# Eight chunks of the feed-forward block in pairs: wider up matmuls, and a Strassen down product with its outputs turned by VectorE

## The chip, the cores and the metric

The kernel runs on one core of one Trainium2 chip. The time is the device time of one execution in microseconds (us). A core has TensorE (PE, matrix products; its loads of stationary data are listed as PEld), VectorE (DVE), ScalarE (ACT), GpSimd (POOL) and SyncE (SP), which here issues every DMA transfer. Each engine works through its own list of instructions in the order of the program; between engines they wait for one another through semaphores. PSUM is the memory that TensorE writes to; the kernel uses it as four pairs of banks, each tile a pair [128, 2, 512].

## What is computed

The reference is a recurrent attention block followed by a feed-forward block, all in float32:

```python
# r, k, v, w, a, b: (B, H, S, D) = (4, 8, 768, 40)
for t in range(S):
    y[:, :, t] = r_t @ state                       # per batch and head, state is 40 x 40
    Sa = state @ a_t
    state = state * w_t - outer(Sa, b_t) + outer(v_t, k_t)
x = y.transpose(0, 2, 1, 3).reshape(3072, 320)     # tokens x (heads * D)
h = x @ w_in                                       # w_in: 320 x 2048
g = h / (1 + exp(-1.702 * h))
out = g @ w_out                                    # w_out: 2048 x 320
```

The two products of the last block are called up (x @ w_in) and down (g @ w_out).

## The kernel before

The sequence is cut into 12 chunks of 64 time steps. A chunk with one half of the batch (two of the four batch rows) is a unit, so there are 24 units. For a unit, `decay`, `prep`, `inverse` and `solve` turn the recurrence over 64 steps into small matmuls. The slowest part is `inverse`: five levels, each a group of matmuls into `ps_level` (L752), a copy of the result to W by ACT or DVE (L763), a subtraction to E by DVE (L765), a 32x32 block transpose to ES by DVE (L714), and a spread of ES into EX (L719 and L721, on ACT, DVE or POOL), from which the next level's matmuls read. The state goes from chunk to chunk.

When both units of a chunk are done, its outputs go through a DRAM tile and come back as xT (320 features on partitions, 256 tokens in the free direction). Then `mlp` (L987) does the chunk's feed-forward part. *Up*: w_in is stationary, the 256 tokens move; a result tile holds two blocks of 128 hidden features, and one ACT instruction (L1000) applies the gelu to all of it and writes g. *Down*: 64 tokens of g are stationary, 320 columns of w_out move, accumulated over 16 blocks of 128 hidden features; the two banks hold the partial sums of the two partition halves, and ACT or DVE copies the first to ob (L1024), DVE adds the second (L1026), and SP sends 64 rows of 1280 bytes per transfer (L1023). Every matmul uses one 64x64 quadrant of TensorE, and `QUARTERS` lists the four quadrants, so that four matmuls form a group. `mm` (L303) issues every matmul, `transfer` (L333) every DMA; so all matmuls have the line L303 and all transfers L333 in the profile.

Nothing is scheduled by the framework. `Plan.add` records tasks with the engines that may take them and their estimated cost in ns, their reads, writes and buffers. A planner that is not part of the file has put them into one order, which stands in the source as the text `ORDER`: each word is a task's number, its engine (p, a, d, g, s) and its PSUM pair. `Plan.listed` (L89) checks that order against the dependencies and issues the tasks in it. The order within each engine, and the engine of each task, are therefore fixed in the text. Feed-forward matmuls stand between the matmuls of the recurrence.

Buffers that matter here: `g` has 4 slots (one chunk: 4 pieces q), `xT` 3, `ob` 1; `extra` is the place through which the raw weights come in at the start, and is free afterwards.

## Time and profile before

| | |
|---|---|
| runs of the kernel before (three) | 680.79, 684.27, 687.98 us; median 684.27 |
| the profiled execution: span, first to last instruction | 680.9 us |
| instructions in the profile | 42,186 |
| DMA | 69.73 MB in 35,312 packets, mean 102 GB/s |
| mean granted TensorE clock over the span | 0.987 |

The profile is of one execution, whose time is its span; outside of it the page shows nothing. The median of the runs is 3.4 us above that span. "Busy" is the time in which an engine had at least one instruction under way; matmuls are pipelined, so that a busy PE is not necessarily a full one. The chain of waits starts at the last instruction and goes back step by step to whatever released it. A group of instructions is given with its line, engine, operation, output and inputs, shape and count, then its busy time in us, the mean ns of one, and the idle time before it with what ended most of that. Each float32 matmul of the program leaves two records, so PE's x19488 are 9,744 matmuls.

### The profile page before, as it was taken

To read this page: it belongs to the slowest core of one execution; us is meant where nothing else is said; L and a number is where in the kernel's file an instruction comes from. 1 tells how busy PE (TensorE), PEld (TensorE's weight loads), DVE (VectorE), ACT (ScalarE), POOL (GpSimd) and SP (SyncE) were. 2 spreads that over 40 slices of the span, in tenths; PEclk is the share of its full clock that TensorE was granted. 3 is DMA by queue.
4 is the path that set the end of the run, shared out by engine and by line. 5 is a ranking of instruction groups with operands and counts; after the bars stand their busy time and mean duration, and the time that the engine had idled before them with its cause. 6 is when DMAs were issued, how large, how long until landed. Compare 5 with 4: busy or idle time off the path is not lost.

```text
span 680.9 us, 42186 instructions
## 1 busy us (share of the span) xinstructions
PE 651.5 (96%) x19488; PEld 561.8 (83%) x19488; DVE 452.8 (66%) x912; ACT 328.9 (48%) x682; POOL 175.4 (26%) x204
## 2 busy tenths in 40 slices
PE   5677999999999999999999999999999999999997
PEld 4666998787999788888888898798888799898785
DVE  5686789767867758858776687768666766675001
ACT  3665845644554754574445455455354354262110
POOL 5442345224123223223213221222412320300000
PEclk9977999999999999999999999999999999999999
DMA  7875563415314414432404513513412411200100
GB/s 218 275 245 148 180 203 110 142 42 152 110 36 130 129 33 120 125 115 71 126 13 126 150 38 108 153 35 106 145 33 70 121 53 42 73 13 23 51 12 20
DMA packets 35312, 69.73 MB, mean 102 GB/s; under 512 B 5440, under 2 KB 14656, under 8 KB 35136
## 3 DMA queue, kind: packets, MB, share of 16 engines
q1 hardware_dynamic: 35136, 67.03, 32.7%
q8 instruction: 153, 2.51, 1.5%
q14 instruction: 23, 0.19, 0.1%
HBM read 59.15 MB, written 7.86 MB: 98 GB/s over the span
## 4 chain that ended last, share of the span: by engine, by line
PE 90%; DMA 5%; DVE 2%; ACT 1%; issue 1%; SPq 1%; ACTq 0%; DVEq 0%
PE ps_up L303 30%; PE ps_down L303 30%; PE ps_level L303 8%; PE ps_y L303 5%; PE ps_B L303 4%; PE ps_X L303 3%; PE ps_N L303 2%; PE ps_rz L303 1%; PE ps_RV L303 1%; PE ps_A L303 1%; DMA w_sb<-in_w_in 1%; PE ps_zT L303 1%; PE ps_cum L303 1%; DMA rv<-in_rv 1%; DMA b<-in_b 1%
## 5 line engine op out<-in xcount | busy, mean ns | idle before, releaser
L303 PE MATMUL ps_up<-xT_all,w_sb 64*64 64x256 f32 x3840 | 249.4, 377 | 0.2 <-PE ps_rz L303 0.2
L303 PE MATMUL ps_down<-w_sb,g 64*64 64x320 f32 x3072 | 239.7, 430 | 0.2 <-ACT zr L881 0.2
L303 PEld LDWEIGHTS ps_up<-xT_all,w_sb 64*64 64x64 f32 x3840 | 168.3, 133 | 15.7 <-PE ps_rz L303 0.3
L303 PEld LDWEIGHTS ps_down<-w_sb,g 64*64 64x64 f32 x3072 | 135.5, 133 | 36.7 <-ACT zr L881 0.4
L1000 ACT ACTIVATE g<-ps_up 128x1024 f32<-128x1024 f32 x48 | 49.2, 1024 | 46.1 <-PE ps_up L303 45.6
L721 POOL TENSOR_TENSOR EX<-ES,quads 128x512 f32<-128x512 f32 x30 | 39.7, 1325 | 118.2 <-DVE ES L714 78.4
L763 ACT COPY W<-ps_level 128x512 f32<-128x512 f32 x56 | 32.7, 585 | 66.8 <-PE ps_level L303 65.2
L303 PEld LDWEIGHTS ps_level<-W,EX 64*64 64x64 f32 x2560 | 57.7, 134 | 6.2 <-DVE T L842 0.2
L765 DVE TENSOR_TENSOR E<-two,ps_level 128x256 f32<-128x256 f32 x80 | 33.1, 415 | 34.4 <-ACT W L763 29.7
L303 PE MATMUL ps_level<-W,EX 64*64 64x64 f32 (+1 forms) x2560 | 54.6, 217 | 0.0
L719 ACT ACTIVATE EX<-ES,quads 128x256 f32<-128x256 f32 x82 | 37.2, 501 | 31.7 <-DVE ES L714 31.3
L303 PEld LDWEIGHTS ps_level<-PT,EX 64*64 64x64 f32 x1280 | 32.0, 144 | 12.0 <-DVE EX L735 3.5
L631 POOL TENSOR_TENSOR ak<-ak,FT 128x512 f32<-128x512 f32 x17 | 22.1, 1299 | 76.7 <-DMA ak<-in_ak 49.8
L303 PE MATMUL ps_level<-PT,EX 64*64 64x64 f32 (+2 forms) x1280 | 34.0, 240 | 7.4 <-DVE EX L735 5.0
L714 DVE STREAM_TRANSPOSE ES<-E 128x256 f32<-128x256 f32 x80 | 35.3, 443 | 4.4
L303 PE MATMUL ps_y<-M,bh 64*64 64x104 f32 (+1 forms) x768 | 35.9, 252 | 1.1 <-issue 0.8
L303 PE MATMUL ps_y<-RV,kh 64*64 64x104 f32 (+1 forms) x768 | 36.2, 253 | 0.7 <-DVE M L919 0.5
L903 ACT COPY B<-ps_B 128x416 f32<-128x416 f32 (+1 forms) x35 | 17.2, 492 | 33.4 <-PE ps_B L303 33.2
L303 PEld LDWEIGHTS ps_y<-RV,kh 64*64 64x64 f32 x768 | 29.2, 137 | 3.2 <-DVE M L919 1.3
L919 DVE TENSOR_TENSOR M<-ps_X,later 128x832 f32<-128x832 f32 (+1 forms) x24 | 23.9, 994 | 11.3 <-PE ps_X L303 10.5
L303 PEld LDWEIGHTS ps_y<-M,bh 64*64 64x64 f32 x768 | 27.8, 137 | 1.8 <-issue 1.2
L303 PE MATMUL ps_B<-RV,A 64*64 64x104 f32 (+1 forms) x768 | 28.5, 250 | 0.4 <-issue 0.3
(133 smaller groups left out, 1085.3 us busy)
## 6 DMA issues: line engine op xcount, KB each, us to landing
ak<-in_ak SPq DMA_DIRECT2D x48, 160.0 KB
rv<-in_rv SPq DMA_DIRECT2D x48, 160.0 KB
time<-in_time SPq DMA_DIRECT2D x24, 320.0 KB
xT_all<-x_dram SPq DMA_DIRECT2D x48, 160.0 KB
wc<-in_wc SPq DMA_DIRECT2D x20, 264.0 KB
logw<-in_w SPq DMA_DIRECT2D x24, 160.0 KB
RV<-in_v SPq DMA_DIRECT2D x24, 160.0 KB
b<-in_b SPq DMA_DIRECT2D x48, 80.0 KB
```

Source lines behind the costliest of these rows:

```text
L303: nc.tensor.matmul(o, lhsT, rhs, start=start, stop=True, skip_group_check=True)
L631: plan.add(R, {"DVE": 690.0, "POOL": 1270.0, "sbuf": True}, lambda t: of(t.engine).tensor_mul(ahT(), ahT(), FT_of(i)), reads=T("ak", "FT") ...
L714: plan.add(rank, dve(256), lambda t: nc.vector.transpose(ES(n), source(t)), writes=[key("ES", n, 6)], **reads)
L719: nc.scalar.activation(dst[:, :, h], ES(n), ACT.Copy, scale=quads[:, h, :1])
L721: of(t.engine).tensor_mul(dst, ES(n).unsqueeze(2).to_broadcast([128, 8, 2, 32]), quads.unsqueeze(1).to_broadcast([128, 8, 2, 32]))
L763: plan.add(rank, any2(512), lambda t: copy(t.engine)(tiles_of(W(n + 1)), blocks(psum(t, ""), 64)), writes=[key("W", n + 1, 5)], pair=pair)
L765: plan.add(rank, dve(256), lambda t: nc.vector.tensor_sub(tiles_of(E(n + 1)), every(two32, [128, 2, 4, 32]), blocks(psum(t, ""), 64)[:, :, ...
L903: plan.add(R, any2(4 * wide), lambda t: copy(t.engine)(dst(), some(psum(t, "")[:, :, :208])), writes=[("Bv", i)] if x and c > 0 else T("B" ...
L919: plan.add(R + 1, dve(8 * wide), lambda t: nc.vector.tensor_tensor(M_of(i)[:, :, :wide].rearrange("p (j b) n -> p b j n", b=2), some(psum( ...
L1000: plan.add(-45, {"ACT": 1030.0, "table": "gelu"}, lambda t: nc.scalar.activation(g_of(c * NQ + q).rearrange("p m r n -> p r m n"), psum(t, ...
```

## The change

Chunks 3 to 10 are taken in pairs (3, 4), (5, 6), (7, 8) and (9, 10); chunks 0, 1, 2 and 11 are done singly as before.

- *Up* (`rise`): in a pair the two chunks' 512 tokens move past the same stationary block of w_in, in one matmul of 512 columns; a result tile holds one block of 128 features for two chunks, and the number of gelu instructions is the same.
- *Down* (`fast_down`): w_out is stationary and the tokens move, so that the result comes out with output columns on partitions. The 256 first output columns (two blocks of 128), the 1,024 + 1,024 hidden features and the two chunks' 256 + 256 tokens form 2x2 blocks, and the product of these is done in Strassen's scheme in Winograd's form: seven products of blocks (P1 to P7) in place of eight. It needs four sums of blocks of w_out, made once (`w_sums`, in `extra`), and four sums of blocks of g for every pair (T1 to T4, in place in g, four pieces each). Partial sums that are wanted on the way (e1, e3, U2, U3, W) are taken out of PSUM while the next product goes on accumulating in the same place. The last 64 output columns (`outer`, P0) are an ordinary product for both chunks.
- The five result tiles [128, 256] of a pair are combined (`combine`), turned by DVE in 32x32 blocks into places of g that are no longer needed, and sent with eight transfers each, every one with 32 partitions of 4 pieces of 32 numbers (128 bytes).
- g becomes one tile with 8 slots, ob has 2 slots, Y is new; `loose` lets a task of the pair of banks wait for its first matmul only, with its other dependencies given by name; the scratch for dynamic DMA is made smaller.
- `ORDER` is a new text for all tasks. In it some of the recurrence's tasks stand on another engine than before.

The diff, without ORDER and cut to its core:

```diff
+    GROUPS = [(0,), (1,), (2,), (3, 4), (5, 6), (7, 8), (9, 10), (11,)]
...
-                     A=1, B=1, RV=2, E0=2, W0=2, P21=2, PT=2, W=2, E=2, ES=2, EX=2, T=2, Tc=1, QT=1, zraw=2, zT=1, M=2, x=1, xT=3, g=4, ob=1), 4)
+                     A=1, B=1, RV=2, E0=2, W0=2, P21=2, PT=2, W=2, E=2, ES=2, EX=2, T=2, Tc=1, QT=1, zraw=2, zT=1, M=2, x=1, xT=3, g=8, Y=1, ob=2), 4)
...
+    w_sums = extra[:, :4 * NF * 64].rearrange("p (k q f n) -> p k q f n", k=4, q=NQ, f=2)
+    Y_more = extra[:, 4 * NF * 64:4 * NF * 64 + 4 * 256].rearrange("p (k n) -> p k n", k=4)
+    w_part = lambda m, n: w_out_sb.rearrange("p (q m f n) -> p q m f n", q=NQ, m=2, f=2)[:, :, m, :, 128 * n:128 * n + 128]
...
     def weights():
         for n in range(len(raws)):
             weight(n, RANKS[n], w_in[n] if n < NQ else w_out[n - NQ])
+
+        every = [("weight", n) for n in range(len(raws)) if n >= NQ or raws[n] in "ab"]
+        for k, (fn, one, two) in enumerate((("add", w_part(0, 1), w_part(1, 1)), ("subtract", w_sums[:, 0], w_part(0, 0)),
+                                            ("subtract", w_part(0, 0), w_part(0, 1)), ("subtract", w_part(1, 0), w_sums[:, 1]))):
+            plan.add(50, {"DVE": 1240.0, "POOL": 2500.0, "sbuf": True}, lambda t, k=k, fn=fn, one=one, two=two: of(t.engine).tensor_tensor(
+                out=w_sums[:, k], in0=one, in1=two, op=getattr(ALU, fn)),
+                     reads=every + ([("wsums", k - 1)] if k == 1 else [("wsums", 1)] if k == 3 else []), writes=[("wsums", k)])
...
-    g_of = lambda n: buf("g", n, [128, 2, 2, 256])
+    g_all = single("g_all", [128, plan.slots["g"], 2, 2, 256])
+    g_turn = {c: c for one in GROUPS for c in one}
+    for one in GROUPS:
+        if len(one) == 2 and (one[0] % 3 < one[1] % 3) != (one[0] % 2 == 0):
+            g_turn[one[0]], g_turn[one[1]] = one[1], one[0]
+    turn_of = {c: n for n, one in enumerate(GROUPS) for c in one}
+    g_no = lambda c, q: g_turn[c] * NQ + q
+    g_of = lambda n: g_all[:, n % plan.slots["g"]]
...
+    def rise(group):
+        c, both = group[0], len(group) == 2
+        R = 10000 + 100 * c
+        xs = [("xs", (n, p)) for n in group for p in BITS]
+        x_at = sorted(n % 3 for n in group)
+        x_of = lambda k: xT_all[:, x_at[0]:x_at[-1] + 1:max(1, x_at[-1] - x_at[0])].rearrange("p s (q k n) -> p s q k n", q=2, n=128)[:, :, :, k]
+        spots = lambda q: sorted(g_no(n, q) % plan.slots["g"] for n in group)
+        g_to = lambda q: g_all[:, spots(q)[0]:spots(q)[-1] + 1:max(1, spots(q)[-1] - spots(q)[0])]
+
+        def up(q, m, k):
+            at, pair = (0, ("up", (c, q, m))) if both else (m * 256, ("up", (c, q, 0)))
+
+            def go(t):
+                ph, x = psum(t, "ps_up"), x_of(k)
+                for r, h in QUARTERS:
+                    mm(ph[HALF[h], r, at:at + 256 * len(group)].rearrange("p (s q n) -> p s q n", q=2, n=128),
+                       w_in_sb[HALF[r], 2 * q + m, k, h * 64:(h + 1) * 64], x[HALF[r]], at == 0 and k == 0)
+            plan.add(R + q, pe((1, 256 * len(group))), go, reads=xs + [("weight", q)],
+                     uses=[("xT", n) for n in group], room=[("g", g_no(n, q)) for n in group], pair=pair, most=1)
+
+        def gelu(q, m):
+            def go(t):
...
+                if both:
+                    nc.scalar.activation(g_to(q)[:, :, m].rearrange("p s r n -> p r s n"), ps.rearrange("p r (s n) -> p r s n", s=2), ACT.Gelu_apprx_sigmoid)
+                else:
+                    nc.scalar.activation(g_to(q)[:, 0].rearrange("p m r n -> p r m n"), ps.rearrange("p r (m n) -> p r m n", m=2), ACT.Gelu_apprx_sigmoid)
+            plan.add(-45, {"ACT": 1030.0, "table": "gelu"}, go, writes=[("g", g_no(n, q)) for n in group],
+                     pair=("up", (c, q, m)))
...
+        for q in range(NQ):
+            for m in BITS:
+                for k in range(NK):
+                    up(q, m, k)
+                if both:
+                    gelu(q, m)
+            if not both:
+                gelu(q, 0)
...
-        def up(q, m, k):
-            def go(t):
-                ph, x = psum(t, "ps_up"), xT_of(c)[:, :, k]
-                for r, h in QUARTERS:
-                    mm(ph[HALF[h], r, m * 256:(m + 1) * 256], w_in_sb[HALF[r], 2 * q + m, k, h * 64:(h + 1) * 64], x[HALF[r]],
-                       m == 0 and k == 0)
-            plan.add(R + q, pe((1, 256)), go, reads=[("xs", (c, p)) for p in BITS] + [("weight", q)],
-                     uses=[("xT", c)], room=[("g", c * NQ + q)], pair=("up", c * NQ + q), most=1)
-
-        def gelu(q):
-            plan.add(-45, {"ACT": 1030.0, "table": "gelu"}, lambda t: nc.scalar.activation(
-                g_of(c * NQ + q).rearrange("p m r n -> p r m n"), psum(t, "").rearrange("p r (m n) -> p r m n", m=2),
-                ACT.Gelu_apprx_sigmoid), writes=[("g", c * NQ + q)], pair=("up", c * NQ + q))
-
...
-        for q in range(NQ):
-            for m in BITS:
-                for k in range(NK):
-                    up(q, m, k)
-            gelu(q)
...
+    def fast_down(c, serial):
+        R = 10000 + 100 * c
+        no = lambda q: (g_no(c, q), g_no(c + 1, q))
+        block = lambda k, n: lambda q: g_of(no(q)[n])[:, k]
+        B11, B12, B21, B22 = block(0, 0), block(0, 1), block(1, 0), block(1, 1)
+        raw = lambda m, n: lambda q: w_part(m, n)[:, q]
+        made = lambda k: lambda q: w_sums[:, k, q]
...
+        Y = lambda k: ob_of(2 * turn_of[c] + k)[:, :256] if k < 2 else buf("Y", serial, [128, 256]) if k == 2 else Y_more[:, k - 3]
+        outs = [("Y", serial), *(("ob", 2 * turn_of[c] + p) for p in BITS)]
...
+        def add(q, key, dst, one, two, reads):
+            plan.add(-46, {"DVE": 697.0, "POOL": 1290.0, "sbuf": True}, lambda t: of(t.engine).tensor_sub(dst(q), one(q), two(q)),
+                     reads=[*of_g(q), *((x, (c, q)) for x in reads)], writes=[(key, (c, q))])
+
+        def times(rank, name, at, left, right, reads, q):
+            def go(t):
+                ps = psum(t, "ps_down")
+                for f in BITS:
+                    for r, h in QUARTERS:
+                        mm(ps[HALF[h], r, 256 * at[1]:256 * at[1] + 256], left(q)[HALF[r], f, h * 64:(h + 1) * 64], right(q)[HALF[r], f],
+                           name == "P1" and q == 0 and f == 0)
+            plan.add(R + rank + 0.1 * q, pe((2, 256)), go, reads=[*of_g(q), *((x, (c, q) if x[0] == "T" else c) for x in reads), *(ready if q == 0 else [])],
+                     writes=[(name, (c, q)), (name, c)], pair=(at[0], c), loose=True, most=1)
+
+        def outer(q, m):
+            def go(t):
...
+                        n = 4 * q + 2 * m + f
+                        mm(ps[HALF[h], r, 256:512], w_out_sb[HALF[r], n * DM + 256:(n + 1) * DM], g_of(no(q)[h])[HALF[r], m, f],
+                           q == 0 and m == 0 and f == 0)
+            plan.add(R + 8 + 0.1 * q, pe((2, 256)), go, reads=[*of_g(q), *(ready if q == 0 else [])], writes=[("P0", (c, q)), ("P0", c)],
+                     pair=("dz", c), loose=True, most=1)
...
+        def evacuate(name, at, k, last, onto=None):
+            ps = lambda t, r: psum(t, "")[:, r, 256 * at[1]:256 * at[1] + 256]
+            if onto is None:
+                plan.add(-45, any2(256), lambda t: copy(t.engine)(Y(k), ps(t, 0)), reads=[(last, c), *ready], room=outs,
+                         writes=[(f"{name}0", c)], pair=(at[0], c), loose=True)
+            else:
+                plan.add(-45, dve(256), lambda t: nc.vector.tensor_add(Y(k), ps(t, 0), Y(k)), reads=[(last, c), (onto, c)],
+                         writes=[(f"{name}0", c)], pair=(at[0], c), loose=True)
+            plan.add(-45, dve(256), lambda t: nc.vector.tensor_add(Y(k), ps(t, 1), Y(k)), reads=[(f"{name}0", c)],
+                     writes=[(name, c)], pair=(at[0], c), loose=True)
+
+        def combine(name, k, fn, one, two, reads):
+            plan.add(-45, {"DVE": 436.0, "POOL": 750.0, "sbuf": True}, lambda t: of(t.engine).tensor_tensor(out=Y(k), in0=Y(one), in1=Y(two), op=fn),
+                     reads=[(x, c) for x in reads], writes=[(name, c)])
+
+        s1, s2, s3, s4 = ("dx", 0), ("dx", 1), ("dz", 0), ("dz", 1)
+        each = range(NQ)
+        for q in each:
+            for m in BITS:
+                outer(q, m)
+            times(10, "P1", s1, raw(0, 0), B11, [], q)
+        for q in each:
+            times(9, "P3", s3, made(3), B22, [], q)
+            times(11, "P2", s2, raw(1, 0), B21, [], q)
+        evacuate("M3", s4, 4, "P0")
+        evacuate("e3", s3, 5, "P3")
+        evacuate("e1", s1, 0, "P1")
+        for q in each:
+            add(q, "T1", B12, B12, B11, ["P0"])
+            times(12, "P5", s3, made(0), B12, ["T1", "e3"], q)
+            add(q, "T2", B22, B22, B12, ["T1", "P3"])
+            times(13, "P6", s1, made(1), B22, ["T2", "e1"], q)
+        evacuate("C11", s2, 0, "P2", "e1")
+        evacuate("U2", s1, 1, "P6")
+        for q in each:
+            add(q, "T3", B11, B22, B11, ["T2", "P1"])
+            times(14, "P7", s1, made(2), B11, ["T3", "U2"], q)
+        evacuate("W", s3, 6, "P5")
+        evacuate("U3", s1, 2, "P7")
+        for q in each:
+            add(q, "T4", B21, B21, B22, ["T2", "P2"])
+            times(15, "P4", s1, raw(1, 1), B21, ["T4", "U3"], q)
+        combine("C12", 1, ALU.add, 1, 6, ["U2", "W"])
+        combine("D", 2, ALU.subtract, 2, 5, ["U3", "e3"])
+        combine("C22", 2, ALU.add, 2, 6, ["D", "W"])
+        evacuate("C21", s1, 3, "P4")
+        ty = lambda k: (B22(3) if k == 4 else B12(3 - k // 2))[:, k % 2]
+        places = [("C11", 0, 0, 0), ("C12", 1, 0, 1), ("C22", 2, 1, 1), ("C21", 3, 1, 0), ("M3", 4, 2, None)]
+        for n, (name, k, block_of, chunk) in enumerate(places):
+            plan.add(-45, dve(256), lambda t, k=k: nc.vector.transpose(ty(k), Y(k)), reads=[(name, c), ("P5", c), ("P6", c), *((x, (c, q)) for x in ("T2", "T3", "T4") for q in each)],
...
+            def store(t, k=k, block_of=block_of, chunk=chunk):
+                for a in range(4):
+                    at_c, col = (c + chunk, 128 * block_of + 32 * a) if chunk is not None else (c + a // 2, 256 + 32 * (a % 2))
+                    for h in BITS:
+                        at_s = at_c * C + 32 * h
+                        to = out.rearrange("(g s) d -> s g d", g=4)[at_s:at_s + 32, :, col:col + 32]
+                        transfer(t, to, ty(k)[32 * a:32 * a + 32].rearrange("p (g h i) -> p g h i", g=4, i=32)[:, :, h])
+            plan.add(-100, {"SP": 2800.0}, store, reads=[("t" + name, c)], uses=[*of_g(2), *of_g(3)], size=128 * 256 * 4)
...
-            mlp(i // 2)
+            for group in GROUPS:
+                if group[-1] == i // 2:
+                    rise(group)
+                    if len(group) == 2:
+                        fast_down(group[0], [one for one in GROUPS if len(one) == 2].index(group))
+                    else:
+                        mlp(group[0])
...
-    nc = bacc.Bacc("TRN2", target_bir_lowering=False, num_devices=1)
+    nc = bacc.Bacc("TRN2", target_bir_lowering=False, num_devices=1, dynamic_dma_scratch_size=1024)
```

291 lines of the change are left out of this document (147 added, 144 removed).

## The prediction

> **What bounds the kernel now.** I read the profile page first: who is busy, and who ends last.
>
> ```profile
> PE 651.5 (96%) x19488; PEld 561.8 (83%) x19488; DVE 452.8 (66%) x912; ACT 328.9 (48%) x682; POOL 175.4 (26%) x204
> ...
> PE 90%; DMA 5%; DVE 2%; ACT 1%; issue 1%; SPq 1%; ACTq 0%; DVEq 0%
> PE ps_up L303 30%; PE ps_down L303 30%; PE ps_level L303 8%; PE ps_y L303 5%; PE ps_B L303 4%; PE ps_X L303 3%; PE ps_N L303 2%; PE ps_rz L303 1%; PE ps_RV L303 1%; PE ps_A L303 1%; DMA w_sb<-in_w_in 1%; PE ps_zT L303 1%; PE ps_cum L303 1%; DMA rv<-in_rv 1%; DMA b<-in_b 1%
> ```
>
> TensorE carries 90% of the chain that ended last, and the two products that the change rewrites carry 30% each. A busy PE need not be a full one, so I went on to the chain in order of time, and to the engines in equal stretches.
>
> ```profile
> 657.75 4.32 PE ps_up L303 x80
> 662.07 14.02 PE ps_down L303 x208
> ```
>
> ```profile
> 0.00:100.00 100.00, 76.89 (x2488) 71.02 (x2492) 72.10 (x116) 58.12 (x139) 42.17 (x64) 0.91 0.69 213
> ...
> 200.00:300.00 100.00, 100.00 (x3091) 85.83 (x3087) 73.57 (x147) 56.70 (x121) 28.76 (x28) 1.00 0.34 101
> 300.00:400.00 100.00, 100.00 (x3052) 84.31 (x3047) 70.79 (x149) 51.18 (x93) 24.41 (x28) 1.00 0.33 98
> 400.00:500.00 100.00, 100.00 (x3100) 86.84 (x3096) 71.53 (x151) 47.94 (x103) 25.14 (x27) 1.00 0.34 102
> ```
>
> The chain gives undisturbed prices. Each matmul in the program is two records, and four of them (one per 64x64 quadrant) run side by side: one group is eight records. So an up group of 256 columns takes 4.32/10 = 0.432 us and a down group of 320 takes 14.02/26 = 0.539 us. The slope is 0.107/64 = 1.67 ns per column and the fixed part 4 ns: nothing is to be had from fewer, longer matmuls, only from fewer columns. The stretches (columns: length, PE, PEld, DVE, ACT, POOL, granted clock, DMA share, GB/s) show PE full from 100 us on at clock 1.00. Summing the starts of successive groups against these prices, PE lost some 36 us before 75 us, while the first transfers land, and only 7 us in all the rest. DVE, the next engine, stands at 71 to 74%. So the kernel is bound by matmul columns from 75 to 676 us, and what is taken from PE there shows at once, as long as DVE keeps up.
>
> **The change on PE.** Per pair of chunks, before: 2 chunks x 2 halves x 16 groups of 320 columns = 64 x 0.539 = 34.5 us of down. After: seven products of 8 groups and the 64 outer columns as 16 groups, 72 groups of 256 = 72 x 0.432 = 31.1 us. That is 3.4 us saved, 13.6 us for four pairs. Up: 80 groups of 256 become 40 of 512; at 4 + 512 x 1.67 = 0.860 us each they save 4 ns per merged group, 160 groups: 0.6 us. The other matmuls are the same in number and shape. Both orders begin alike (PE's first 120 rows, DVE's first 114, SP's first 60), so the 36 us of the start stay, and both end with a single chunk's down and the same last store. **PE: minus 14.2 us**, if it stays fed.
>
> **The change on DVE.** The rows to price it with:
>
> ```profile
> L721 DVE TENSOR_TENSOR EX<-ES,quads 128x512 f32<-128x512 f32 x29 | 20.1, 695 | 0.9
> ...
> L965 DVE TENSOR_TENSOR x<-zr,FT 128x128 f32<-128x128 f32 x56 | 20.1, 418 | 0.2
> ...
> L636 DVE TENSOR_TENSOR ak<-ak,GT 128x512 f32<-128x512 f32 x12 | 11.0, 920 | 2.6 <-DMA ak<-in_ak 2.5
> ```
>
> ```profile
> L714 DVE STREAM_TRANSPOSE ES<-E 128x256 f32<-128x256 f32 x80 | 35.3, 443 | 4.4
> L765 DVE TENSOR_TENSOR E<-two,ps_level 128x256 f32<-128x256 f32 x80 | 33.1, 415 | 34.4 <-ACT W L763 29.7 <-PE ps_level L303 3.8
> ```
>
> New on DVE, by the changed order: 57 of the 64 subtractions T1 to T4 (128x512, as EX: 0.695) 39.6 us; 36 additions out of PSUM and 3 copies (128x256, as E: 0.415) 16.2; 20 transposes (0.443) 8.9; 5 combinations (as E) 2.1; four sums of weights (128x1024, twice EX) 5.6. Gone: 16 additions and 8 copies of ob (0.483 and 0.490), 11.6. Together +61 us. The new order also moves old work from POOL and ACT to DVE: EX spreads 29 to 65 (+25.0), x 56 to 92 (+15.0), ak products 19 to 31 (+11.0), T spreads 6 to 11 (+3.7), the rest about -20 (40 small copies of Tc at 0.214 and 7 of W at 0.682 go to ACT, among others). Together +35. DVE goes **from 453 to some 549 us**, and POOL's instructions from 204 to 147.
>
> Where it lies decides. The chunks' pairs stand between PE's work marks 50 and 525 us (marks count matmul time alone; 525 is the last matmul of the recurrence, which stood at 571 before, so it is also packed closer). In this stretch I priced every instruction by its row's median, in the order in which the program lists them over all engines. That order can be trusted for this: in the trace of before, DVE's instructions start within about a microsecond of the place it gives them. Between the marks PE has 475 us of work and DVE 456 us, 96%. In before it was 521 and 383, 73%. Cut into 25 us of PE work, DVE has more than PE in seven pieces of nineteen (27.8, 25.3, 27.4, 26.8, 25.4, 27.0, 27.7), in sum 12 us more; in before no piece exceeds 21.3. Each such piece is a wait of PE, because the recurrence (matmul, copy, transpose, spread, next matmul) runs through DVE and PE's queue is in order: behind a level's matmul that waits for its EX stand the up and down groups that would have filled the gap. Pieces of 50 us, as if engines could run far ahead, leave 3 us; pieces of 10 us 18, of 5 us 30 (before: 0, 1, 3). **I take +12**, since before's DVE never ran more than about a microsecond ahead, but waits of a few hundred ns did vanish. Bounds 3 and 30.
>
> **The stores.** A pair's outputs now leave as 40 transfers of 32x4x32 in place of 8 of 64x320, all on SP's queue.
>
> ```profile
> L333 SPq DMA_DIRECT2D out<-ob x48: 467/564/1412, 118.7 to 677.7; - x48
> ```
>
> At 0.564 us each (minimum, median, maximum in the row) a burst holds SP for 22.6 us. Queued behind it: after the first pair the loads of rv, ak and b, with 10 to 33 us of PE work until their first use; after the second pair logw and wc of a later unit, with 10 us, so they come some 4 us late to ACT's logarithm, and the gelus behind that on ACT come late with it; after the last pair, the turned outputs lie in buffers of g that the last chunk's gelus want back 22 to 25 us of PE work after the first store, just about when the last has landed. A new shape may be issued faster (loads of 40 rows: 0.29) or slower; from 0.6 us on each further 0.1 us costs the end 4 us. **I take +2**, bounds 0 and 10. Each transfer is made of 128-byte pieces, 20,480 in all; the mean piece of before costs an engine 101 ns (32.7% of 16 x 680.9 us over 35,136 pieces), which would be 32 us of each engine per pair, no more than its idle share (DMA 0.34) in the 100 us that a pair lasts. A page speaks against these stores: the Trainium skill, "DMA: Bandwidth & Descriptors", Specifications, asks for 512 bytes or more per piece for line rate, and says that smaller ones are read, modified and written. No run here shows it yet; by the rows above it would be rival C. Where the sum takes the page at its word, +2 becomes +10.
>
> **Sum.** 680.9 - 14.2 + 12 + 2 = 680.7 us for the profiled span. The runs of before lie at 680.79, 684.27 and 687.98, so the span of the profile is at their lower end, 3.4 us (0.5%) under the median; against the median the sum gives **684 us, no change**. About 1% (6.8 us) is what a measurement of this kernel tells from no change.
>
> **Rivals.**
> A, *DVE's backlog spreads out*: neighbouring pieces with room absorb it, as the 50 us pieces allow (3 us), and SP is fast enough. For it: PE lost only 7 us in 600 so far, and DVE's total still fits. Against it: before had a quarter of DVE free, here 4%. 684 - 14.2 + 3 = **673 us**.
> B, *DVE becomes the bound of the middle*: at 96% asked for, it cannot lose time to its own waits on PE and ACT. It decides from the point where DVE's busy share of the stretch falls under 456/489 = 93%: from there the waits exceed the 14.2 us gained. No stretch of the trace has DVE above 79% (39.6 of the 50 us from 100 to 150). With the 5 us pieces: 684 - 14.2 + 30 = **700 us**.
> C, *the stores*: their small pieces or their issue delay loads and the last chunk's gelus, 684 - 14.2 + 12 + 10 = **692 us**.
> That PE's saving itself fails would need groups of 512 or of the turned products to cost more than linear; the counts are fixed by the program and both forms are plain moving columns, so I give it no chance of its own.
>
> **How the numbers follow.** Forecast 0.44 (677.5 to 691), A 0.28, B 0.21, C 0.07. Faster by over 1% is A, 0.28; within it 0.44; slower B and C, 0.28. The range must reach into A and B until a tenth is out on each side: 670 to 699.
>
> **What the next profile would show.** ps_down groups at 0.432 us and fewer of them, ps_up at 0.860, and PE's sum 14 us smaller: the first step. DVE near 549 us, over 90% busy in stretches between 100 and 560 us, with PE idle there put down to DVE (EX, ES, T, the additions of L1118): the second; PE full throughout would make A right. SP's row for out<-g_all at about 0.56 us, and a last gelu that waits for out<-g_all or not: the third. The forecast is wrong if DVE's busy time is well off 549, if PE loses under 5 or over 20 us in the middle, or if the new start differs from the old.

## The result and the profile after

The changed kernel takes 730.2 us (median of four runs, 726.45 to 731.61) where the kernel before takes 683.97 on the same chip: 1.065 times as long, 95% interval 1.059 to 1.071. The forecast was 684 with a range from 670 to 699. In what follows, "over before" is (ratio - 1) x 684 us; the change stands at **+44.5 us** (40 to 49) on that scale.

The page of the changed kernel: busy time of each engine, and the chain that ended last by engine and by line.

```profile
PE 662.3 (91%) x18464; PEld 495.3 (68%) x18464; DVE 518.7 (71%) x1044; ACT 330.6 (45%) x719; POOL 121.9 (17%) x147
...
PE 73%; DVE 9%; ACT 5%; DMA 4%; issue 4%; SPq 4%; POOL 0%; ACTq 0%; DVEq 0%
PE ps_down L300 24%; PE ps_up L300 23%; PE ps_level L300 7%; PE ps_y L300 4%; PE ps_B L300 4%; SPq L330 4%; PE ps_X L300 2%; PE ps_N L300 2%; DMA b<-in_b 1%; PE ps_rz L300 1%; DVE g_all L1086 1%; PE ps_RV L300 1%; ACT W L771 1%; PE ps_A L300 1%; DVE ES L722 1%
```

TensorE's part of the chain fell from 90% to 73%. The rest is now spread over VectorE (9%), ScalarE, transfers and SP's queue (4%, 1% before). The prices of TensorE's groups are as forecast; the chain's end shows them undisturbed (start, length, what):

```profile
688.33 2.16 PE ps_up L300 x40
690.49 0.86 PE ps_down L300 x16
691.35 2.16 PE ps_up L300 x40
```

Five groups of 256 columns in 2.16 us are 0.432 each, two of a turned product in 0.86 are 0.43, and six groups of 512 columns in a row from 645.7 us on took 5.15 us, 0.858 each. So TensorE got its 14 us less of work, and lost far more. The two kernels between 100 and 600 us, before first (columns: length, PE, PEld, DVE, ACT, POOL, granted clock, DMA share, GB/s):

```profile
100.00:600.00 500.00, 498.51 (x15310) 426.95 (x15306) 358.40 (x740) 252.29 (x514) 131.96 (x139) 1.00 0.31 93
```

```profile
100.00:600.00 500.00, 462.04 (x13564) 350.22 (x13559) 397.66 (x822) 243.52 (x529) 75.63 (x77) 0.99 0.33 90
```

PE stands still for 38 of the 500 us, although VectorE is at 80% only, and no 50 us of the trace has it above 88%. Busy time still flatters PE. With the prices of its groups, each stretch can be split into up and down products, recurrence products, and time lost (us, to about 2 us):

| stretch | before: up and down, recurrence, lost | changed |
|---|---|---|
| 75 to 150 | 49.6, 22.4, 3.1 | 40.1, 25.7, 9.3 |
| 150 to 250 | 64.0, 33.9, 2.1 | 53.6, 35.3, 11.0 |
| 250 to 350 | 64.8, 34.4, 0.8 | 56.9, 36.0, 7.0 |
| 350 to 450 | 66.0, 33.5, 0.5 | 55.0, 28.7, 16.3 |
| 450 to 550 | 64.6, 33.3, 2.2 | 53.6, 28.9, 17.4 |
| behind the recurrence's last matmul | 47.5 | 78.5 |
| in all | 413.6, 214.5 | 399.3, 214.5 |

Two things stand in it. First, the losses of 350 to 550 us are large, and much of them sits in two places. TensorE's longest waits between 75 us and the end (engine, line, waited for; us in all, times, longest):

```profile
PE ps_N L300 <- DVE ak L639: 6.8, 1, 6.8
PE ps_B L300 <- ACT zr L889: 6.1, 1, 6.1
```

The first one in stretches of 5 us, with the columns as above:

```profile
390.00:395.00 5.00, 4.46 (x80) 1.87 (x80) 2.06 (x7) 2.74 (x7) 0.00 (x0) 1.00 0.22 31
395.00:400.00 5.00, 0.13 (x4) 0.00 (x0) 0.00 (x0) 0.00 (x0) 0.00 (x0) 0.91 0.45 138
400.00:405.00 5.00, 3.08 (x57) 2.19 (x61) 2.97 (x7) 0.37 (x1) 0.00 (x0) 0.50 0.07 19
405.00:410.00 5.00, 5.00 (x152) 4.00 (x148) 2.97 (x7) 3.04 (x10) 1.29 (x1) 0.91 0.08 20
```

All engines are empty from 395 to 400 us. SP had been sending a pair's outputs from 371.5 to 395.2 us, 40 transfers in a row; only then did it issue the load of ak, which landed at 400.4, and the recurrence went on. When PE came back, its granted clock was 0.50. The second stop, at 505 us, is the same with wc. Secondly, the losses begin at 75 us, where no pair's output exists yet: there each stretch has some 10 us less of up and down products in it, and 31 us of them (78.5 - 47.5) are found behind the recurrence's last matmul. (The expectation of e10 below goes by 36.6 and 77.5 us, which leaves out the first block of each.) In the kernel before, the recurrence's last matmul starts at 628.4 us, and from 628.64 up and down products run without a stop to 676.09 us; the chain of before begins that stretch with these:

```profile
628.64 10.78 PE ps_down L303 x160
639.42 4.32 PE ps_up L303 x80
643.73 2.15 PE ps_down L303 x32
```

### The profile page after: what moved, and what is told of

It is laid out like the page before. It is cut to its first block, busy times and chain, and to the rows that moved or that the text cites. A ratio compares the mean times of both kernels' runs of the same rounds, so it can differ in the third digit from the quotient of the medians.

```text
span 729.3 us, 40391 instructions
## 1 busy us (share of the span) xinstructions
PE 662.3 (91%) x18464; PEld 495.3 (68%) x18464; DVE 518.7 (71%) x1044; ACT 330.6 (45%) x719; POOL 121.9 (17%) x147
## 4 chain that ended last, share of the span: by engine, by line
PE 73%; DVE 9%; ACT 5%; DMA 4%; issue 4%; SPq 4%; POOL 0%; ACTq 0%; DVEq 0%
PE ps_down L300 24%; PE ps_up L300 23%; PE ps_level L300 7%; PE ps_y L300 4%; PE ps_B L300 4%; SPq L330 4%; PE ps_X L300 2%; PE ps_N L300 2%; DMA b<-in_b 1%; PE ps_rz L300 1%; DVE g_all L1086 1%; PE ps_RV L300 1%; ACT W L771 1%; PE ps_A L300 1%; DVE ES L722 1%
## 5 line engine op out<-in xcount | busy, mean ns | idle before, releaser
L300 PE MATMUL ps_up<-xT_all,w_sb 64*64 64x256 f32 (+1 forms) x2560 | 247.6, 488 | 3.7 <-issue 3.5
L300 PEld LDWEIGHTS ps_up<-xT_all,w_sb 64*64 64x64 f32 x2560 | 104.4, 134 | 48.2 <-issue 35.0
L300 PE MATMUL ps_down<-w_sb,g_all 64*64 64x320 f32 x1024 | 81.3, 431 | 0.9 <-issue 0.6
L300 PE MATMUL ps_down<-g_all,w_sb 64*64 64x256 f32 x1280 | 80.4, 377 | 0.9 <-issue 0.7
L300 PE MATMUL ps_down<-g_all,extra 64*64 64x256 f32 x1024 | 64.3, 378 | 4.9 <-DVE extra L1118 2.7
L771 ACT COPY W<-ps_level 128x512 f32<-128x512 f32 x63 | 36.6, 585 | 61.0 <-PE ps_level L300 57.3
L300 PEld LDWEIGHTS ps_down<-g_all,w_sb 64*64 64x64 f32 x1280 | 49.3, 133 | 16.1 <-issue 3.1
L300 PEld LDWEIGHTS ps_down<-w_sb,g_all 64*64 64x64 f32 x1024 | 45.4, 133 | 15.8 <-issue 1.8
L1026 ACT ACTIVATE g_all<-ps_up 128x1024 f32<-128x1024 f32 x32 | 32.7, 1024 | 49.1 <-PE ps_up L300 42.2
L1086 DVE TENSOR_TENSOR g_all<-g_all 128x512 f32<-128x512 f32 x57 | 40.8, 740 | 18.6 <-PE ps_down L300 18.3
L300 PEld LDWEIGHTS ps_down<-g_all,extra 64*64 64x64 f32 x1024 | 40.0, 133 | 18.3 <-DVE extra L1118 3.2
L729 DVE TENSOR_TENSOR EX<-ES,quads 128x512 f32<-128x512 f32 x65 | 47.6, 732 | 1.6
L300 PE MATMUL ps_y<-RV,kh 64*64 64x104 f32 (+1 forms) x768 | 36.6, 255 | 2.1 <-issue 1.6
```

The costliest lines, as they stand in the source:

```text
L300: nc.tensor.matmul(o, lhsT, rhs, start=start, stop=True, skip_group_check=True)
L729: of(t.engine).tensor_mul(dst, ES(n).unsqueeze(2).to_broadcast([128, 8, 2, 32]), quads.unsqueeze(1).to_broadcast([128, 8, 2, 32]))
L771: plan.add(rank, any2(512), lambda t: copy(t.engine)(tiles_of(W(n + 1)), blocks(psum(t, ""), 64)), writes=[key("W", n + 1, 5)], pair=pair)
L1026: nc.scalar.activation(g_to(q)[:, :, m].rearrange("p s r n -> p r s n"), ps.rearrange("p r (s n) -> p r s n", s=2), ACT.Gelu_apprx_sigmoid)
L1086: plan.add(-46, {"DVE": 697.0, "POOL": 1290.0, "sbuf": True}, lambda t: of(t.engine).tensor_sub(dst(q), one(q), two(q)), reads=[*of_g(q), ...
```

## The experiments

The theories, as they stood ahead of the first four: *stores* (SP's bursts make the two stops), *vector* (VectorE's longer queue makes the many small ones), *grain* (the 512-column groups hold others up), *order* (TensorE's order leaves the recurrence no time, whatever VectorE does).

### One transfer for each turned tile; subtractions made small; both; up in two halves

```diff
# e1
-                for a in range(4): ...  for h in BITS: transfer(t, to, ty(k)[32 * a:32 * a + 32]...[:, :, h])
+                transfer(t, out[n * S + c * C:n * S + c * C + 128, :256], ty(k))     # fifth tile: [128, 4, 64]
# e2
-  of(t.engine).tensor_sub(dst(q), one(q), two(q))
+  of(t.engine).tensor_sub(dst(q)[:, :, :4], one(q)[:, :, :4], two(q)[:, :, :4])
# e3: both
# e4, in the pairs
-  mm(ph[HALF[h], r, at:at + 256 * len(group)]..., x[HALF[r]], ...)
+  for s in range(len(group)): mm(ph[HALF[h], r, at + 256 * s:at + 256 * s + 256]..., x[HALF[r], s], ...)
```

Expected of e1:

> Edit: each turned tile of a pair goes out in one transfer of 128 pieces of 1 KB (the fifth: of 256 bytes), 5 transfers a pair in place of 40, to places of the output that are not the right ones; all arithmetic stays. Store theory: SP's bursts of 23.7 us (40 transfers of 0.43 us and the gaps between them, in the changed kernel's trace) cause the two long stops of TensorE at 394 and 504 us, 6.8 and 6.3 us of waiting, each followed by some 5 us at a granted clock of 0.50, so 9.5 + 8.4 us, and part of what follows at 524 us (3 us) and 355 us (3 us): 730 falls to 706 to 714 and both stops go. Vector theory: the stores are a symptom, the time stays within 3 us of 727.

Expected of e2:

> Edit: the 64 subtractions of Strassen's scheme on GELU's outputs (T1 to T4) are made on 8 of their 512 columns; the work left out is the rest of these subtractions. Everything keeps its place. Vector theory: VectorE's queue is the cause of the 45 us of small stops of TensorE between 100 and 700 us; 57 subtractions of 0.74 us there become some 0.07 us, 38 us less on VectorE, which takes its sum back to 480 from 519 us: 730 falls to 700 to 712. Store theory: no more than 5 us of it, since SP's bursts keep their place. Order theory (TensorE's order as written leaves the recurrence no time, whatever VectorE does): within 5 us of 730.

Expected of e3:

> Both edits together: one transfer for each turned tile, and the subtractions on 8 of 512 columns (the rest of them left out). If stores and VectorE are the two causes, the sum of both gains: 680 to 692. If either one alone is the cause, this equals the better of the two runs within 4 us. Order theory: stays above 700.

Expected of e4:

> Edit: in the pairs the up product goes out as two matrix products of 256 columns in place of one of 512, with the same weights loaded for each; same tasks in the same places. Grain theory (long products hold up what stands behind them, or the 512-column form itself waits): some 10 us or more are won back. Vector and store theories: the price alone, 4 pairs x 64 groups x (0.864 - 0.860 us), under 2 us either way, and TensorE's loads grow by 1280 of 0.134 us, which lie beside its products.

| | us | ratio, 95% interval | over before |
|---|---|---|---|
| changed kernel | 730.2 | 1.065 (1.059 to 1.071) | +44.5 |
| e1, one transfer a tile | 703.4 | 1.029 (1.023 to 1.036) | +20.0 |
| e2, small subtractions | 716.9 | 1.051 (1.045 to 1.056) | +34.5 |
| e3, both | 698.0 | 1.022 (1.017 to 1.028) | +15.0 |
| e4, up in halves | 733.5 | 1.074 (1.069 to 1.080) | +50.8 |

In e1 both long stops are gone; VectorE does the same work as before the edit (page, and TensorE's longest wait after 75 us):

```profile
PE 657.0 (93%) x18464; PEld 488.5 (69%) x18464; DVE 518.2 (73%) x1044; ACT 330.7 (47%) x719; POOL 121.9 (17%) x147
```

```profile
PE ps_down L300 <- DVE extra L1118: 2.7, 1, 2.7
```

So the way in which the outputs were stored costs 24.5 us (about 6 either way, from the two intervals). The gain is a little larger than the store theory's 706 to 714. The subtractions are worth 10 us by themselves, but 5 on top of e1 (the intervals of e1 and e3 overlap): 31 us of VectorE's time (518 to 487) for 5 us, far from what the vector theory asked. None of the three expectations of e2 holds: 716.9 lies between the 712 of the vector theory and the 725 that the two others allow. Grain falls: halving the groups brings nothing back (a pair has 40 of them, not the 64 of the expectation). And e3's 698.0 meets none of its three expectations, if narrowly: it is not the 680 to 692 us of two causes that make up the whole, it is 5 and not 4 us from e1, and it is not above 700. 15 us over before (11 to 19) stay, where 14 less than before were due. 29 us had no owner yet, and e3's table looked like that of the changed kernel up to 250 us (6.6 and 10.2 us lost, with 42.2 and 52.6 us of up and down products).

### The recurrence nearly alone

A new theory, *pace*: the recurrence is a chain of steps through TensorE, ScalarE and VectorE, and needs nearly all the time that it has. Up and down products between its steps are then almost free, and those behind its end cost their full length.

```diff
# e5, kernel before; e6 likewise, with times() at q == 0, f == 0 and outer() at q == m == f == 0
-  for r, h in QUARTERS:                                  # up
+  for r, h in QUARTERS if k == 0 else []:
-  for f in (2 * m, 2 * m + 1):                           # down
+  for f in (2 * m, 2 * m + 1)[:m == 0]:
```

Expected of e5:

> Edit on the kernel before: the up product takes the first of its five parts of the input features alone, the down product the first of 16 blocks of the hidden features; four fifths of the up products and fifteen sixteenths of the down products are left out, about 359 of the 414 us that up and down hold on TensorE at full rate. All else, GELU, copies and stores too, stays, and so does the order. What is left is the recurrence at its own pace. Pace theory (the recurrence's chain of VectorE, ScalarE and TensorE steps needs nearly the time that it has, so taking products from between its steps brings little): its last product, at 628 us in the kernel before, comes at 540 us or later, and the run takes 560 us or more. Filling theory (TensorE's work sets the time and the chain has ample slack): the run falls to the sum of VectorE's work and the start, 480 us or less.

Expected of e6:

> The same on the changed kernel: one fifth of the up products, one eighth of the down products of the pairs (one sixteenth of the turned one) and one sixteenth of the others are made, the rest is left out; all work of VectorE, ScalarE and the stores stays. Pace theory: the last recurrence product, at 644 us in the changed kernel, comes at 570 us or later and the run takes over 590 us, that is 20 us or more longer than the kernel before under the same cut, by the load of VectorE (519 for 453 us) and the bursts of stores. If VectorE and the stores cost the recurrence nothing by themselves, both cut kernels end within 10 us of each other.

Measured: 599.5 us (0.882, 0.875 to 0.888) for the kernel before and 669.3 us (0.984, 0.975 to 0.994) for the changed one. 359 of TensorE's us were taken from the kernel before, and 80 came back. The last recurrence matmul moved from 628 to 573 us, and from 644 to 623 in the changed kernel. VectorE, with nothing to hold it up but the chain itself (e5, then e6):

```profile
100.00:200.00 100.00, 68.21 (x2210) 55.30 (x2207) 82.09 (x168) 58.34 (x121) 33.48 (x35) 0.81 0.39 114
200.00:300.00 100.00, 72.17 (x2406) 60.10 (x2402) 77.33 (x161) 58.25 (x121) 29.99 (x28) 0.81 0.34 104
```

```profile
100.00:200.00 100.00, 72.24 (x2232) 60.58 (x2232) 84.52 (x167) 54.78 (x124) 23.64 (x23) 0.69 0.40 116
200.00:300.00 100.00, 70.69 (x2237) 56.80 (x2227) 79.50 (x169) 52.82 (x117) 14.55 (x15) 0.78 0.30 94
```

It gets to 77 to 85% in these stretches. That is not a limit of VectorE: in e3 it was busy for 45.85 of the 50 us from 100 to 150. One reservation: the granted clock fell to 0.81 and 0.69 to 0.78 here, so the recurrence's own matmuls ran slower than in the full kernels, and 573 us is more than the chain needs at full clock. The two later edits at the kernel before do not have this fault (clock 0.99 and 1.00).

```diff
# e11: e6 with the edits of e1 and e2
```

Expected:

> The changed kernel with its up and down products cut as in the earlier cut run (669 us), and in addition one transfer for each turned tile and the subtractions on 8 of 512 columns; the rest of these is left out. The kernel before under the same cut takes 599 us. If stores and subtractions are what made the recurrence of the changed kernel slower, 605 to 625. If it is rather the wait of a pair's products for both chunks and the work behind the last step (48 us behind it here, 26 in the kernel before), 640 or more.

Two executions, 620.1 and 629.7 us, and no interval: the first lies in the range of the store and subtraction theory, the second between the two. By the first, the stores and the subtractions are 49 of the 70 us between the two cut kernels, by the second 40; 21 to 30 us are left. Behind the last recurrence matmul e11 has 28 us in the profile of its longer execution (600 to 628), e5 26 (573 to 599); so nearly all of what is left is time that the recurrence itself takes longer in the new order, with few products in it and at a lower clock (0.78 for 0.82). What in the new order does that was not tried.

### Steps back on their old engines; stores on GpSimd

```diff
# e7, on e3: 258 words of ORDER, for example
-  ... 503d ... 567d ...
+  ... 503a ... 567g ...
# e8, on the changed kernel: 20 words of ORDER from s to g, and
-  transfer(t, to, ty(k)[32 * a:32 * a + 32]...)
+  nc.gpsimd.dma_start(to, ty(k)[32 * a:32 * a + 32]...)
```

Expected of e7:

> Edit on the kernel with one transfer a tile and the subtractions on 8 of 512 columns (the rest of them left out; 698.0 us): in addition the 258 small steps of the recurrence that the new order gives to another engine than the old one go back to the old one, at the same places of the order (56 from VectorE to GpSimd, 76 from VectorE to ScalarE, the others from ScalarE or GpSimd). Moved-work theory: VectorE loses some 35 us, and of the 29 us that still part 698 from 684 - 14 = 669 some 10 to 20 come back: 678 to 688. Pace theory (less of the up and down products stands between the recurrence's steps, since a pair waits for both its chunks): within 6 us of 698, either way, since the steps of the chain are as long as before or longer on GpSimd (1.33 for 0.73 us).

Expected of e8:

> Edit on the changed kernel: the 40 transfers of a pair's outputs are issued by GpSimd (17% busy) in place of SP; same transfers, same places of the order. If it is SP's time that the transfers cost (and not their 128-byte pieces), the two long stops go and 730 falls to 702 to 712, as with one transfer a tile (703.4). If it is the small pieces at the DMA engines or in memory, it stays above 722. Rival: issuing costs GpSimd so much that the recurrence's steps on it (122 us) come late: above 730.

e7 takes 724.7 us (1.065, 1.059 to 1.071), 29 us more than e3: neither theory's figure. Its last recurrence matmul comes at 637 us instead of 611. But the edit took little off VectorE, 480 us for 487 in e3 where 35 us less had been expected: 132 steps left it and 108 others came to it, and what stayed got slower (the 40 scans 908 ns for 684, b 825 for 707) with GpSimd busy for 185 us in place of 114. So the run does not decide whether the load on VectorE was the harm. It shows that, at the places of the new order, the new engines are better by 29 us than the old ones. The steps that moved to GpSimd take longer there (EX 1.31 us for 0.72), and VectorE's share of the chain that ended last went from 12% to 22%, GpSimd's from 0% to 2%; which of the 258 steps did it was not tried.

e8 takes 735.6 us (1.079, 1.073 to 1.086): nothing gained, as both the second expectation (the small pieces) and the third (GpSimd's own steps) allow. The chain of waits around 370 us speaks for the third (start, length, what):

```profile
370.32 4.51 POOL out L1168 x8
374.83 0.02 issue
374.85 0.74 POOL Y L1122
375.58 3.08 POOL out L1168 x6
...
380.59 0.68 POOL PT L717
...
381.31 0.70 PE ps_level L300 x14
```

The burst moved to another in-order queue, and there the recurrence's step PT stood behind it, as the load of ak had on SP. An engine that is busy 17% of the time was no free place, because what it does lies on the chain. Against the second stands the profile's page: issued by GpSimd, the 160 transfers go in 5,120 packets in place of 20,480, and those of 128 bytes are gone (packets of the changed kernel, then of e8):

```profile
DMA packets 55785, 69.61 MB, mean 95 GB/s; under 512 B 27968, under 2 KB 35136, under 8 KB 55616
```

```profile
DMA packets 37866, 69.62 MB, mean 95 GB/s; under 512 B 7488, under 2 KB 17216, under 8 KB 37696
```

### Less work on TensorE, and the same work at another place

```diff
# e9, kernel before: the last of 16 blocks left out
+  for f in (2 * m, 2 * m + 1)[:1 + (m < NM - 1)]:
# e10, kernel before: 4 of 16 left out in chunks 0 to 10, 44 more in chunk 11
+  for f in (2 * m, 2 * m + 1)[:1 + (m < NM // 2)] if c < 11 else (2 * m, 2 * m + 1, *(2 * m,) * (6 if m < NM // 2 else 5)):
```

Expected of e9:

> Edit on the kernel before: the last of the 16 blocks of the hidden features is left out of every down product, so TensorE has 24 x 0.539 = 12.9 us less to do, about what the change takes from it, and nothing else moves, no engine has more to do, the order is the same. If TensorE's work sets the time (the first term of the prediction), the kernel before gets 11 to 13 us faster: 666 to 670. Pace theory: the recurrence's steps come no sooner, so only a part comes back, by the cut kernels some 80 us for 359 us taken out, plus the 1.1 us after the last step: 2 to 7 us.

Expected of e10:

> Edit on the kernel before: chunks 0 to 10 leave 4 of the 16 blocks of their down products out (11 x 2 x 4 x 0.539 = 47.4 us less between the recurrence's steps), and the last chunk, which stands behind the last of these steps, makes the same number of products again on its own data (47.4 us more). TensorE's sum, the other engines and the order are unchanged; the outputs are not the reference's. It stands for what the pairs do to the order: 36.6 us of up and down products behind the last step in the kernel before, 77.5 us in the changed one. If TensorE's work alone sets the time: 682, as before. Pace theory: the 47.4 us come in full at the end, and of the 47.4 us taken from the middle only 10 to 25 come back: 704 to 720.

e9: 673.5 us, 0.990 (0.987 to 0.992), that is 7.1 us (5.3 to 8.9) back for 12.9 taken, **0.55 of it**, just over the upper edge of what the pace theory gave. e10: 709.0 us, 1.043 (1.040 to 1.045), **+29.1 us** (27 to 31) with the same sum on TensorE, the same vector work and the same stores. Of the 88 groups left out, 8 stood behind the recurrence's last matmul already, so 43.1 us were moved from ahead of it to behind it, and 0.67 of that is lost. That matmul comes at 610 us, 18 earlier than in the kernel before, although 43 us of products are gone from ahead of it. TensorE of the kernel before never stands still for long, yet it loses time as soon as it is given less (e10, 100 to 600 us):

```profile
100.00:600.00 500.00, 482.11 (x15212) 408.29 (x15208) 367.72 (x775) 262.29 (x531) 133.09 (x140) 1.00 0.32 93
```

18 us of stops here, where the kernel before has 1.5, and VectorE at 74%: it is not a full engine alone that holds the time, but with it a chain whose slack the products had just covered. "Almost free" was too much all the same: of what is taken out from between the steps, about half comes back (e9), or 18 of 43 us (e10).

e3, the changed kernel with light stores and subtractions, can be laid beside e10: it has 45 us less of up and down products ahead of the recurrence's last matmul than the kernel before (321 for 366), and that matmul comes 17 us earlier (611 for 628).

### Bursts in the kernel before, and a burst on two queues

```diff
# e12, kernel before, chunks 4, 6, 8, 10
-  transfer(t, out[o:o + C, :], ob_of(serial)[HALF[b]])
+  for n in range(10): transfer(t, out[o:o + C, 32 * n:32 * n + 32], ob_of(serial)[HALF[b], 32 * n:32 * n + 32])
# e13, changed kernel: of the transfers with h = 0 and h = 1
+  if h: nc.gpsimd.dma_start(to, from_)
+  else: transfer(t, to, from_)
```

Expected of e12:

> Edit on the kernel before: the outputs of chunks 4, 6, 8 and 10 go out in pieces of 32 columns, 40 transfers a chunk in place of 4, so SP issues as many more as in the changed kernel (144 more, some 62 us of SP at 0.43 us), in bursts of 20, half as long as a pair's; same pieces of 128 bytes. Burst theory (what counts is who stands behind a burst of 20 us and more on SP): at most 8 us slower, since a burst takes some 9 us. If each small transfer has its price wherever it stands: about 25 us slower, as the changed kernel gained from doing without them.

Expected of e13:

> Edit on the changed kernel: of each turned tile's eight transfers SP issues four and GpSimd four, so a pair's burst of 40 on one queue (23.7 us on SP alone, 24 us on GpSimd alone) becomes 20 on each, some 10 to 12 us; same transfers, same pieces, same result. If it is the length of the burst on one in-order queue that costs the 24 us (ratio 1.065 against 1.029 with one transfer a tile), half of it or more comes back, since a wait of 6 us behind a burst shortened by 12 us is gone: ratio 1.035 to 1.052. If each small transfer has its price wherever it is issued: 1.06 to 1.07. Rival: GpSimd's and SP's share of the recurrence are now both held up, once each: above 1.07.

e12 takes 732.5 us, 1.077 (1.074 to 1.079), +52 us: both expectations miss. The bursts were longer than thought, 12.6 to 16 us for 20 transfers (0.595 us each in SP's row, 0.43 had been assumed), but above all something else stood behind them (TensorE's waits, then three stretches around one of them):

```profile
PE ps_up L303 <- DMA xT_all<-x_dram: 31.7, 3, 11.7
```

```profile
452.00:456.00 4.00, 0.00 (x0) 0.00 (x0) 1.76 (x4) 0.91 (x2) 0.00 (x0) 0.79 0.69 204
456.00:460.00 4.00, 0.00 (x0) 0.00 (x0) 0.00 (x0) 0.00 (x0) 0.00 (x0) 0.50 0.59 196
460.00:464.00 4.00, 2.47 (x20) 1.59 (x23) 0.00 (x0) 0.00 (x0) 0.12 (x1) 0.50 0.57 168
```

The recurrence's outputs go through DRAM by the same queue; behind a burst they came 9 to 12 us late, four times, and the up products that wait for them stand in TensorE's queue ahead of everything else. The four stops are 41 us, and the halved clock after them (3 to 6 us each) adds an estimated 9; that is nearly all of the 52. So the number of transfers has no fixed price.

e13 takes 714.5 us, 1.047 (1.045 to 1.049), +32 us. The same 160 transfers, in bursts of some 10 to 15 us on each of two queues, cost 12 of the 24.5 us less: the length of the burst on one queue counts. The ratio lies where the burst's length had put it. The pieces are not all the same as the expectation had it: GpSimd's half goes in 2,560 packets, SP's in 10,240 of 128 bytes. The packets alone do not order the runs, since the run with none of 128 bytes (e8) is the slowest and the one with half of them (e13) the fastest of the three. What makes up the 12 us that e13 is still above e1 was not separated. It is the fastest form of the whole change in these runs, and slower than the kernel before; no run points to one that beats that.

## Why the prediction was wrong, point by point

| term | predicted, us | measured, us |
|---|---|---|
| TensorE's work | -14.2 | work -14.3, of which 0.55 counts (e9): -7.9 |
| up and down products behind the recurrence's end | not seen: 0 | 31.0 more there, of which 0.67 counts (e10): +21 |
| VectorE's load | +12 | subtractions +4.9 (e1 to e3) |
| stores | +2 | +24.5 (changed kernel to e1) |
| sum | -0.2 | +42.5; the kernels differ by +44.5 |

**The step that failed first** is the reading of the bound: "So the kernel is bound by matmul columns from 75 to 676 us, and what is taken from PE there shows at once, as long as DVE keeps up." PE at 100% with little lost was true (7 us by the prediction, 8.7 up to 550 us in the table above). That nothing else was as tight did not follow: the full PE hid a recurrence with hardly any slack, and e9, the plainest form of the sentence, gives 0.55 and not 1.

**The second is a number that the prediction held and passed over:** "525 is the last matmul of the recurrence, which stood at 571 before, so it is also packed closer". 46 us of matmul work less ahead of that point, with 14 less in all, meant that the other 32 stood behind it; 31 were found there. A pair's products wait for both chunks, so the steps of chunks 3 and 4 must be covered by what chunks 0 to 2 left, and 31 us more come at an end where the recurrence no longer runs. That this costs 0.67 of itself is shown in the kernel before (e10). That it does the same in the changed kernel is argued: from e3, whose recurrence ends as much earlier for as much less ahead of it as e10's, from the losses ahead of 250 us, and from the sum of the table, which closes within its errors. Against it stands e11: with the products nearly gone, the new order still makes the recurrence some 20 to 30 us longer, so a part of these 21 us may be the order's own, whatever stands behind the end. The runs do not tell the two apart.

**VectorE.** Its sum is 519 us, not 549. The rows to compare with those of before (page by form of the changed kernel):

```profile
L729 DVE TENSOR_TENSOR EX<-ES,quads 128x512 f32<-128x512 f32 x65 | 47.6, 732 | 1.6
L1086 DVE TENSOR_TENSOR g_all<-g_all 128x512 f32<-128x512 f32 x57 | 40.8, 740 | 18.6 <-PE ps_down L300 18.3
L973 DVE TENSOR_TENSOR x<-zr,FT 128x128 f32<-128x128 f32 x92 | 26.6, 348 | 0.8 <-DMA x_dram<-x 0.7
L644 DVE TENSOR_TENSOR ak<-ak,GT 128x512 f32<-128x512 f32 x14 | 9.5, 682 | 12.2 <-DMA ak<-in_ak 9.6 <-ACT wch L589 2.4
```

The counts were right; x (348 for 418 ns) and ak (682 for 920) came cheaper, the subtractions a little dearer (740 for 695). The prices are worth some 11 of the 30 us. The rest is a step of the sum: it adds up means, while busy time counts instructions that overlap once (durations add up to 484 us before and 570 after, busy time to 453 and 519). The test "over 90% busy" failed: 80% between 100 and 600 us. Rival B forecast 700 us with PE waiting for a full VectorE; the time came out longer, but VectorE was not full, and taking 31 us off it bought 5, so its mechanism is not what the runs show. Summing work by stretches could not see this: it counts what an engine has to do, and the loss lies in steps that wait for one another.

**Stores.** The transfers named as late were the right ones (ak after the first pair, wc after the second, and the last chunk's gelu did wait 9.4 us for out<-g_all), and the issue time was even overrated: 0.43 us at the median where 0.564 was taken. "10 to 33 us of PE work until their first use" held too: PE had work for 23.7 us from the start of the first burst (371.5 to 395.1). What was wrong is what the prediction made of it, +2 with 10 as the upper bound. The burst held SP for just these 23.7 us; behind it rv and ak were issued, ak landed at 400.4, two VectorE steps followed, PE stood still for 6.8 us, and the clock halved. Rival C had the mechanism and less than half the size. The Trainium skill's sentence in "DMA: Bandwidth & Descriptors", Specifications, on pieces under 512 bytes agrees with the trace as to rate: 128 bytes took 13 ns of an engine, 1 KB took 46 in e1, so 0.10 against 0.045 ns per byte. But all 20,480 pieces together are 278 us, 17 of each of 16 engines, and without any of them the time was 1.079 (e8), with half of them 1.047 (e13). So the hold of one queue was the cost, for half of the 24.5 us at least, and the pieces are not seen to be. The Trainium skill, "DMA: Bandwidth & Descriptors", says under "Issuing engines are not separate DMA queues" that issuing from several engines saves the sequencer's issue time and nothing else; e13 is what that saving is worth here, e8 what it is not worth when only the engine changes.

## What to carry to other kernels

An engine at 100% is the bound only if nothing else is as tight: before a gain on it is counted in full, ask how fast the chain of dependent steps would go without it, and leave a little of its work out to measure that. When work that covered a chain is put together in larger lots, look for what it covered and for how much now stands behind the chain's end. Count a transfer's price by what stands behind it on its queue, not by its bytes or its number.

## What the runs showed of the hardware

- After a stop of 6 to 12 us TensorE came back at a granted clock of 0.50 and worked 3 to 6 us before it had 1.00 again, in all six cases (two in the changed kernel, four in e12); a stop of 6.8 us with 4 us at half the clock so costs an estimated 9. A stop of 2.7 us, at 356 us in the changed kernel, left the clock at 1.00. The Trainium skill, "TensorE: Matmul & The Clock Gate", Part 1, has the clock at 4/8 after an idle window of about 3.4 us and back after as long of steady work; the trace agrees. With TensorE stopped often, the mean clock was 0.82 and 0.76 (e5, e6).
- Issuing a store took SP 0.43 us (32 partitions x 4 x 32), 0.564 (64 x 320), 0.595 (64 x 32 columns), and GpSimd 0.548 with hardly any spread; so fewer bytes did not make the issue shorter.
- VectorE's x product took 280 ns at the median in 81 cases that met no GpSimd instruction, and 653 in the 11 that did, 3.03 us at most; this was not looked into further.
